# Two attention and two long-convolution layers on one core: all logits summed by heads, the last convolution's tables asked for earlier, and new orders of work

## The chip, the cores and the metric

The kernel runs on one core of a Trainium2 chip. The core has a matrix engine (TensorE, PE; its weight loads are listed apart as PEld), a vector engine (VectorE, DVE), an activation engine (ScalarE, ACT), a general engine (GpSimd, POOL) and a queue engine (SyncE, SP) that issues most transfers. Each works through its own list of instructions in order and waits on semaphores of the others. PE writes to PSUM, from where DVE or ACT copy to SBUF. The metric is the device time of one execution in microseconds.

## The reference

One sequence of 2048 positions and 512 features passes through four layers: attention A, convolution B, A again, B again, each added to its input after a layer norm. Both A layers use the same weights, both B layers the same filter.

```python
def _A_ref(x, wqkv, wo):            # 32 heads of 16, window W = 8, dilation 2
    qkv = (x @ wqkv).reshape(B, S, 3, H, Dh)...
    idx = pos[:, None] - off[None, :]           # s, s-2, ..., s-14
    logits = einsum("bhsd,bhswd->bhsw", q, kg) * scale    # masked where idx < 0
    o = einsum("bhsw,bhswd->bhsd", softmax(logits), vg)
    return o.reshape(B, S, D) @ wo
def _B_ref(u, ...):                 # K[d, l] = Re sum_n C B dt exp(dt A l)
    y = irfft(rfft(u, 2L) * rfft(K, 2L))[:L]    # causal convolution over L = 2048
    return y + u * Dskip
x = x + A(layernorm(x)); x = x + B(layernorm(x)); x = x + A(layernorm(x)); x = x + B(layernorm(x))
```

## The kernel before

**Stages.** `k_gen` builds the filter K on DVE (tables of powers, L1119) and PE (products, L1277), and beside it runs the first attention's front: layer norm of the input (`apply`, L195 and L197), transposes (L1205), projections of q and k (L1215). `LayerA.core` is an attention; it runs twice. `FftB` is a convolution by a two-stage transform with matmuls; it runs twice, the first time also with the transform of the filter itself. Between the first convolution and the second attention lies a second front (layer norm, transposes L271, projections L282 and L223).

**Order.** Every stage takes its order from a string of letters or tokens written out by hand: `ORDERK` for `k_gen`, `CORE0` and `CORE1` for the two attentions, `ORDER0` and `ORDER1` for the two convolutions, `ORDERF` for the end of the first convolution mixed with the second front. One letter issues one operation with all its instructions, on whichever engines it has; since the engines have lists of their own, a string is the interleaving of four lists. Under `tc.manual_schedule(engines=...)` the listed engines keep the written order. Before the change there were several such stretches, one for a stage, with a few calls between them (`open_mid`, `front_w`).

**An attention.** Rows lie in 16 row blocks `a` of 128; four of them make a block `q`. Letters of the core: `v` values of one row block (four matmuls of 512 columns, L398, ACT copy L400), `q` a projection of q (L223, copy L225), `m` a product q times eight shifted k's on DVE (`mult`, L342, 128 x 4096), `l` its sum over the 16 features of a head on PE (`lsum`), `x` the maximum (L414, DVE), `e`, `r`, `n` exponent, logarithm of the sum and normalised exponent (L430, L443, L453, ACT), `T` a turn (L459 to L461), `P` the weights times eight shifted v's on DVE (L472, 128 x 4096), `S` or `V` the sum of these over the taps on PE (L497 in 64-row halves, L487 whole), `O` the output projection with the residual (L506, L508), `b`, `d`, `a`, `f`, `t` the next layer norm (`a` applies it to a row block on DVE, `f` on ACT).

**Two ways to sum logits.** `NCOL` says how many of the four blocks `q` are summed by heads: the 32 columns of `ind` are the weights, the product is the moving operand, and four such matmuls fill the 32-partition quarters of the PSUM tile `L` (L350, 8 matmuls of 512 columns for one `l`). The result has heads on partitions, so after the normalised exponent the weights must be turned with 8 transposes into the upper half of the same PSUM tile and copied by ACT. The other blocks take the product as weights, 32 of them for one `l`, each with `ind8` of 8 columns as the moving operand (L354); the result has rows on partitions and needs no turn. `NCOL = (2, 2)`: blocks 0 and 1 by heads, 2 and 3 the other way. There are two `L` tiles and two tiles of products (`prod`), so the third product waits until the first has been summed; `ex`, which holds the exponents and is the turn's input, has one tile.

**The end of the filter table.** `ORDERK` ends with the first three logit products of the first attention (`X`, into the freed table tiles) and their sums (`Z`); the fourth product is `m` in `CORE0`, and its tile lies where the tables were. The letters `z` and `y` of `ORDERK` apply the layer norm, on engines named in `ENGK`. `KROWS` names the engines of the eight copies that bring the filter into the layout of the convolution (L1459, letters A to H of `CORE0`).

**The second front.** In `ORDERF`, `v` and `z` are the last pieces of the first convolution's inverse transform into `x_sb` (matmuls with the twiddles `g2`, then an evacuation, L911 to L937), `h`, `H`, `a`, `p`, `n` the statistics and layer norm of a block (`h` half of the columns, `H` all, `a` aggregates, `p` the power on ACT, `n` applies), `T` its transposes, `E` an evacuation of half of them, `P` and `Q` projections, `x` the shifted copy of k. Letter A or D behind it is ACT or DVE. The rest of the front (four P, three Q, the last shifted copies) is issued by four events 0 to 3 in `CORE1`.

**The convolutions.** `K` and `U` are the first transform stage of filter and input (L811, evacuation L800), `k` and `u` the second (L818, L800 and L869), `m` the product of spectra on DVE (L857), `y` or `Y` the first inverse stage (L883 or L887), `w` and `v` the last. The filter's spectra go to `kf_dram` during the first convolution and are read back in the second into a ring of tiles: seven of its own (`kf_ring`) and three more in tiles that the attention frees (`kx`, the rest of `w2_sb`). `w2_sb` holds the second stage's weights, 32 transfers of 128 KB for each convolution, in the place of `kT_ext` and the weights (letter `w`).

## Time and profile before

| | before |
|---|---|
| time, median of 3 runs | 395.1 us (394.6 to 396.57) |
| span of the profiled execution | 393.9 us, first to last instruction |
| DVE busy | 372.8 us in 449 instructions |
| ACT busy | 331.1 us in 568 |
| PE busy | 324.1 us in 6451 matmuls |
| granted PE clock | 0.999 over the span |
| moved by DMA | 54.18 MB, mean 138 GB/s |

The profile is of one execution; its span is 1.2 us shorter than the runs' median, which also holds what lies before the first and behind the last instruction. Times in a view by stage are from the span's start. In a view of groups, a row reads: line, engine, operation, output from input, shapes and count, then busy time and mean ns of one, then the engine's idle time ahead of them and what ended it. In a view in order of time a row reads: start, length, engine, line, operation, count, and in brackets the idle time before it with its releaser; "issue" means that the profile shows nothing that it waited for. Neighbouring instructions of one engine overlap by some tens of ns, and PE's matmuls by more, so the start of the next instruction tells better what one costs than its length.

### The profile page before, as it was taken

The page shows a single profiled execution, that of the slowest core. Times are in us where ns is not written, and L with a number is a line of the kernel's source. Part 1 is how long each engine was busy: PE and PEld are TensorE (multiplying, and loading weights), DVE is VectorE, ACT ScalarE, POOL GpSimd, SP SyncE. Part 2 cuts the span into 40 slices and gives each one's busy share as a digit, 9 for nine tenths or more (in the row PEclk, how much of TensorE's full clock was granted, in tenths as well). Part 3 has the DMA queues.
Part 4 walks back from the last instruction along what each step waited for, and adds up shares of the span by engine and source line. Part 5 has one row for each costly group of instructions (what it writes and reads, how often), then busy time and mean ns, then how long its engine had stood idle before and what let it go on. Part 6 is the DMA issues. An engine that isn't in the chain of part 4 may idle for free.

```text
span 393.9 us, 14769 instructions
## 1 busy us (share of the span) xinstructions
PE 324.1 (82%) x6451; PEld 231.5 (59%) x6499; DVE 372.8 (95%) x449; ACT 331.1 (84%) x568; POOL 65.5 (17%) x97
## 2 busy tenths in 40 slices
PE   3000258999999999999998899999999999998894
PEld 2000116756734676766887888543456676677894
DVE  6999999999989999999999989979999999989984
ACT  7999999997558799899999998574666779889992
POOL 9402960000280000010731201100000020000000
PEclk9999999999999999999999999999999999999999
DMA  7953810414027556277678634820253057604525
GB/s 209 396 155 50 83 53 3 106 28 108 9 66 198 128 168 176 61 228 235 215 265 300 216 110 110 300 62 2 73 141 96 3 170 222 195 13 155 171 68 152
DMA packets 68303, 54.18 MB, mean 138 GB/s; under 512 B 33545, under 2 KB 58670, under 8 KB 67982
## 3 DMA queue, kind: packets, MB, share of 16 engines
q1 hardware_dynamic: 66566, 48.70, 42.7%
q0 software_dynamic: 1664, 4.52, 3.1%
q8 instruction: 51, 0.84, 0.9%
q14 instruction: 14, 0.11, 0.1%
q10 hardware_dynamic: 8, 0.00, 0.0%
HBM read 30.15 MB, written 13.24 MB: 110 GB/s over the span
## 4 chain that ended last, share of the span: by engine, by line
PE 49%; DVE 21%; ACT 19%; issue 5%; DMA 2%; SPq 2%; POOL 1%; DVEq 0%; ACTq 0%; POOLq 0%
PE pq L398 7%; PE po L497 5%; PE pq L508 4%; PE pq L223 4%; PE pk L1277 3%; DVE A_t L1119 3%; ACT ub L869 3%; DVE B_t L1119 3%; PE L L354 3%; PE pp L282 3%; ACT a1s L800 3%; PE pp L1215 2%; DVE t L857 2%; SPq L596 2%; PE L L350 2%
## 5 line engine op out<-in xcount | busy, mean ns | idle before, releaser
L472 DVE TENSOR_TENSOR pav<-attn,v_ext 128x4096 bf16<-128x4096 bf16 (+1 forms) x34 | 72.3, 2160 | 0.3 <-DMA v_ext<-v_ext 0.3
L342 DVE TENSOR_TENSOR prod<-qT,kT_ext 128x4096 bf16<-128x4096 bf16 x29 | 65.6, 2288 | 3.0 <-PE L L350 2.1
L1119 DVE TENSOR_TENSOR A_t<-A_t,pow_t 128x1024 bf16<-128x1024 bf16 (+4 forms) x46 | 38.2, 873 | 0.2
L1205 PE MATMUL pt<-ident,x_blk 128*128 128x128 bf16 x64 | 6.0, 241 | 39.4 <-ACT x_blk L195 39.4
L508 PE MATMUL pq<-wop,oT 128*128 128x512 bf16 x121 | 31.5, 379 | 2.4 <-issue 1.9
L497 PEld LDWEIGHTS <-pav 64*128 64x128 bf16 x1728 | 26.9, 95 | 9.9 <-DVE pav L472 3.3
L869 ACT CAST ub<-pb 128x1024 bf16<-128x1024 f32 x32 | 32.6, 1110 | 0.0
L1215 PE MATMUL pp<-xnT,kT_ext 128*128 128x512 bf16 x88 | 25.5, 413 | 7.3 <-ACT xnT L1208 4.3
L818 PE MATMUL pb<-a1s,w_sb 128*128 128x64 bf16 x768 | 27.4, 193 | 3.8 <-ACT ub L869 1.4
L398 PE MATMUL pq<-wv,xnT 128*128 128x512 bf16 x123 | 30.0, 379 | 0.5 <-ACT kgs L1285 0.3
L497 PE MATMUL po<-ident,pav 64*128 64x64 bf16 x1728 | 29.9, 190 | 0.6 <-ACT oT L499 0.2
L400 ACT CAST v_ext<-pq 128x512 bf16<-128x512 f32 x32 | 18.7, 586 | 13.5 <-PE pq L398 11.1
L800 ACT CAST a1s<-pb 128x1024 bf16<-128x1024 f32 x29 | 28.5, 1063 | 1.2 <-PE pb L811 1.2
L1205 PEld LDWEIGHTS <-x_blk 128*128 128x128 bf16 x64 | 4.6, 107 | 41.3 <-ACT x_blk L195 40.2
L818 PEld LDWEIGHTS <-w_sb 128*128 128x128 bf16 x768 | 25.1, 98 | 6.0 <-issue 4.0
L178 POOL TENSOR_TENSOR ln_rstd<-ln_rstd,ln_mh 128x4 f32<-128x4 f32 x2 | 4.0, 1995 | 120.1 <-DVE ln_rstd L177 66.9
L1277 PEld LDWEIGHTS <-A_t 128*64 128x64 bf16 (+1 forms) x512 | 21.7, 103 | 3.8 <-DVE A_t L1119 0.2
L800 DVE CAST a1s<-pb 128x1024 bf16<-128x1024 f32 x19 | 22.5, 1220 | 1.4 <-PE pb L811 1.0
L1277 PE MATMUL pk<-B_t,A_t 128*64 128x84 bf16 (+1 forms) x512 | 23.5, 201 | 0.2
L223 PE MATMUL pq<-xnT,kT_ext 128*128 128x512 bf16 x85 | 22.6, 379 | 0.9 <-issue 0.5
L225 ACT CAST qT<-pq 128x512 bf16<-128x512 f32 x24 | 14.0, 585 | 9.8 <-PE pq L223 9.5
L398 PEld LDWEIGHTS <-xnT 128*128 128x128 bf16 x128 | 11.9, 97 | 15.3 <-issue 2.4
(264 smaller groups left out, 919.9 us busy)
## 6 DMA issues: line engine op xcount, KB each, us to landing
w_sb<-w_dram SPq DMA_DIRECT2D x64, 128.0 KB, 3.0
w_dram<-xnT SPq DMA_DIRECT2D x1, 4096.0 KB
kf_ring<-kf_dram SPq DMA_DIRECT2D x13, 256.0 KB, 3.8
kf_ring<-kf_dram SPq DMA_DIRECT2D x26, 128.0 KB, 3.6
v_ext<-v_ext SPq DMA_DIRECT2D x4, 784.0 KB, 6.1
x_blk<-in_A_x_dram SPq DMA_DIRECT2D x4, 512.0 KB, 4.7
kT_ext<-in_A_wqkv_dram SPq DMA_DIRECT2D x4, 512.0 KB, 9.2
x_sb<-in_A_x_dram SPq DMA_DIRECT2D x4, 512.0 KB, 6.3
```

What stands on the lines that cost most here:

```text
L223: nc.tensor.matmul(pq[:], lhsT=self.wqk[:, dt, ft * P:(ft + 1) * P], rhs=self.xnT[:, dt, q * 512:(q + 1) * 512], start=(dt == 0), stop=(dt ...
L342: nc.vector.tensor_tensor(pr, self.qT[q][:, ft].unsqueeze(1).to_broadcast([P, W, 4, P]), kap, ALU.mult)
L398: nc.tensor.matmul(pp[:], lhsT=xnT[:, dt, a * P:(a + 1) * P], rhs=wv[:, dt, :], start=(dt == 0), stop=(dt == NDT - 1))
L472: nc.vector.tensor_tensor(pv[:, i], attn[:, n % 4].unsqueeze(2).to_broadcast([P, W, DH // parts, H]), vap, ALU.mult)
L497: nc.tensor.matmul(po[:, h, 0, i * nt + ft, :], lhsT=pvf[rows, i, w, ft * P:(ft + 1) * P], rhs=ident[rows, rows], start=(w == 0 and ft + i ...
L508: nc.tensor.matmul(pw[:], lhsT=oT[:, ftp, :], rhs=self.wo[:, ftp, :], start=False, stop=(ftp == NDT - 1))
L800: (self.nc.scalar.copy if eng == "act" else self.nc.vector.tensor_copy)(dst, src)
L818: nc.tensor.matmul(p2[:, j, :], lhsT=self.w2[:, ec * EC + j, :], rhs=a1s[:, ec * EC + j, :], start=True, stop=True)
L869: nc.scalar.copy(ub[:], p2)
L1119: return lambda: nc.vector.tensor_tensor(*args)
L1215: nc.tensor.matmul(pps[kind, b, ft][:], lhsT=la.wqk[:, dt, c:c + P], rhs=la.xnT[:, dt, b * 512:(b + 1) * 512], start=(dt == 0), stop=(dt = ...
L1277: nc.tensor.matmul(o, lhsT=lhs, rhs=Bt[:, ri, c * CH + ql].rearrange("p b g -> p (b g)"), start=(not half and j % 4 == 0 and ri == 0), sto ...
```

## The change

1. `NCOL` becomes (4, 4): all blocks of both attentions are summed by heads, so `CORE0` and `CORE1` have four `T` instead of two.
2. The last convolution's `g2` and its seven own spectrum tiles are allocated before the second attention on the other side of SBUF, and four events of `CORE1` (0 to 3, behind its second product) issue their 22 transfers. The convolution starts with these seven as loaded.
3. `load_w2` is cut into four parts of eight transfers (letter `W`); in both cores the four stand together.
4. The rest of the second front, four events before, becomes 13 single letters with an engine each (`RKEYS`, `RROWS`); `qproj1`, `front_k` and `front_ext` take the engine.
5. All six order strings are new. Counted by letter: `ENGK` has no application on DVE (two before), `KROWS` has one copy on ACT (three before), `ORDERF` evacuates four transposed halves on ACT (two before), `CORE0` has 5 `a` and 3 `f` (6 and 2), 15 `S` and 1 `V` (13 and 3), `CORE1` 4 `a` and 8 `f` (7 and 5), 16 `S` and no `V` (14 and 2). The evacuations of `ORDER0` and `ORDER1` keep their totals for each engine.
6. One `manual_schedule` for DVE, ACT, PE and SP covers the whole program; POOL is added for `k_gen` as before.

```diff
 ORDERK = """
-sbiCCiCisCGiCbiMsaibsCbMiibMcMsTibMGicGMMbasMGiGibTMTMbsGGTabbiTTiaTsicGTbbacTiTibcGsTMTGiaGaMlM
...
-kUTzkzUkTxkTKttkKkUkUkpKekekxKUUpkkKqxpKUqUUxUkUoEUUkpQkUKkpxUUoxpUXpxXKopxxZXZZ
...
+UqKzkQkqTzKzkUzUkqpxQtUUtpUexkKpUUxUkUeUkKkUxkKpkxEppKoUxoUkkUKoEkUpxkKpXZxXXxZZ
...
 ORDERF = """
-yD h00 h01 yA YA v101A v100A v110A v111A h10 z12A a0 p0 v113A h11 a1 p1 z02A S z03A n0D T0 n1G E00D
-v103D E01A P03 H2 a2 T1 P01 E10D p2 E11D Q00 n2G H3 P00 a3 P02 P11 P12 p3 T2 E21D E20D P10 P13
-P22 P20 n3D T3 E31A P23 P21 E30D x1
+yD yA h00 YA v100A v101A v110A v111A v113A h01 h10 a0 v103D p0 z12A n0D S h11 z02A T0 E01A a1 p1
+z03A E00D n1G P03 P01 H2 P02 T1 E10A a2 p2 E11D P00 P11 P10 Q00 n2G H3 a3 T2 E21D E20A p3 n3D P13
+P22 P12 P21 T3 E30A x1D E31D P23 P20
...
 CORE0 = """
-vmvvvvqlvmxvlmemvvrclvnlmqTlqmxmvvelvvvvcmlqcPlSPrqOmncml1VTxPPqeSmr2lqP4OlSOSm5PqOP3S7lmOSnlPOx
-VPeOPSPrOSnPO6SObbP9SwOP8SPdBHOVaOPfSEdObatSaCaAfataGDFO
+vvmvcmvlcxqmlvevlvmmvrclnqvcmlmTvqlvvvvxvevqlmP1rqlnPq4mmlVxm2TqOPlSm5lS3l7PqOPSPeOSrOmPnSlOTxSP
+eOSbPrOSnO8PSP6TO9SdbOPSOPSPPOWWWWSffdOSbPtaaEODGSAaBCfOtaFHa
 CORE1 = """
-0m1l2ml3mqvvmvllqvmqvxqelmlvmmvvqrlnqlmTvmxPPvlvvqvvqvmlmvqlqelmSrqnxmPSPqTOSOSlePOlPmrSOSnmOOPl
-bSlPSPwOxdfPVaePOSraPOnVabPOSPdOSOPSbPOSfaOftSdafaaftO
+CDABFGJKImmN0123EqHllvLmmvvlmqvlvvqmxqlmlvvemqlrvnlmqxTqmvlvvvmPvvPvqllqemqlmqrSmnOSTxPeOPlSlrSO
+qPSnOPmmbTSPOllWWWWOSxdeOPrSfnPSfPOSPTOSbPOPSdfOPSOSfPbaOSPftOfSdtffaaaO
...
-NCOL = (2, 2)
-ENGK = dict(..., y="AAAAAAAAAADA", z="DAAA", ...)
+NCOL = (4, 4)
+ENGK = dict(..., y="AAAAAAAAAAAA", z="AAAA", ...)
 STATD = (3,)
-KROWS = "DADAADDD"
+RKEYS = "ABCDEFGHIJKLN"
+RROWS = "AADDAADAAADDD"
+KROWS = "DDDDADDD"
...
+def kf_read(nc, kc, kf_dram, n):
+    g, ec = divmod(n, NEC)
+    nc.sync.dma_start(kc[0::2], kf_dram[g, ec])
+    for r in range(2):
+        nc.sync.dma_start(kc[1::2, r], kf_dram[g, ec, :, 1 - r])
...
     def open_mid(self):
-        nc.sync.dma_start(self.g2[:], self.g2_dram[:])
         if t:
-            for n in (4, 3):
-                kr = self.c_mid.enter_context(tc.tile_pool(name=f"b{t}_kf{n}", bufs=1, reuse_waits="tile"))
...
+            self.nkf = len(self.ring)
+            self.kf = dict(enumerate(self.ring))
             self.ring += self.extra
...
+    ctx.enter_context(tc.manual_schedule(engines=MAN))
...
-    with tc.manual_schedule(engines=MAN_ALL):
+    with tc.manual_schedule(engines={ET.Pool}):
         C = k_gen(...)
...
+    ring_ctx = ExitStack()
+    g2p = ring_ctx.enter_context(tc.tile_pool(name="b1_g2", bufs=1, side="right", reuse_waits="tile"))
+    g2 = g2p.tile([P, 2, 16, P], BF16, name="g2_sb")
+    ring = []
+    for n in (4, 3):
+        kr = ring_ctx.enter_context(tc.tile_pool(name=f"b1_kf{n}", bufs=1, side="right", reuse_waits="tile"))
...
-        ev = {"w": lambda: la.load_w2(w2_dram),
-              "0": last(("P", 3, 0), ("P", 3, 1), ("x", 0), ("x", 2), ("P", 3, 2), ("Q", 0, 1), ("e", 0), ("Q", 0, 2)),
-              "1": last(("P", 3, 3), ("Q", 0, 3)), "2": last(("e", 1), ("e", 2)), "3": last(("e", 3))}
+    ev = la.w2_loads(w2_dram)
+    ev |= {"0": lambda: nc.sync.dma_start(g2[:], g2_dram[:]), "1": lambda: ring_loads(0, 1), "2": lambda: ring_loads(2, 3),
+           "3": lambda: ring_loads(4, 5, 6)}
+    rest = (("P", 3, 0), ("P", 3, 1), ("x", 0), ("x", 2), ("P", 3, 2), ("Q", 0, 1), ("e", 0), ("Q", 0, 2),
+            ("P", 3, 3), ("Q", 0, 3), ("e", 1), ("e", 2), ("e", 3))
+    for c, e, (op, *ix) in zip(RKEYS, RROWS, rest):
+        ev[c] = lambda e=e, op=op, ix=ix: front[op](*ix, dict(A="act", D="dve")[e])
+    la.core(x_sb, u, lnp, CORE1, ev)
```

More of the change, by code (lines that the diff above doesn't have):

```diff
@@ L217, in __init__, with qproj1 @@
         self.st = [dict() for _ in range(4)]
-    def qproj1(self, q, ft, qT, ps, tag):
+    def qproj1(self, q, ft, qT, ps, tag, eng="act"):
         nc = self.nc
@@ L846, in kf_load @@
         kc = self.ring[n % len(self.ring)]
-        sync.dma_start(kc[0::2], self.kf_dram[g, ec])
-        for r in range(2):
-            sync.dma_start(kc[1::2, r], self.kf_dram[g, ec, :, 1 - r])
+        kf_read(self.nc, kc, self.kf_dram, n)
         self.kf[n] = kc
@@ L1487 @@
     fb.open_mid()
-    with tc.manual_schedule(engines=MAN):
-        late["."] = lambda: None
-        fb.run(ORDER0, u, k=kp, late=[late[c] for c in LATE0.split()])
+    late["."] = lambda: None
+    fb.run(ORDER0, u, k=kp, late=[late[c] for c in LATE0.split()], more={"g": lambda: nc.sync.dma_start(fb.g2[:], g2_dram[:])})
     fb.c_mid.close()
@@ new lines @@
+    fb.run(ORDERF, None, more=front)
+    la.front_close()
+    fb.c_ps.close()
+    fb.c_grp.close()
+    krctx.close()
+    ring_ctx = ExitStack()
[4 more added lines that the diff above has]
+        kr = ring_ctx.enter_context(tc.tile_pool(name=f"b1_kf{n}", bufs=1, side="right", reuse_waits="tile"))
+        kr = kr.tile([P, n, 2, DQG, EC], BF16, name=f"kf_ring{n}")
+        ring += [kr[:, i] for i in range(n)]
```

128 lines of the change are left out of this document (61 added, 67 removed).

## The prediction

> **What bounds the kernel now.** I read the page first (busy times and the chain of waits), then busy time by stage, then the groups with their shapes kept apart, then the order in time at the places where VectorE (DVE) waits.
>
> ```profile
> PE 324.1 (82%) x6451; PEld 231.5 (59%) x6499; DVE 372.8 (95%) x449; ACT 331.1 (84%) x568; POOL 65.5 (17%) x97
> ...
> PE 49%; DVE 21%; ACT 19%; issue 5%; DMA 2%; SPq 2%; POOL 1%; DVEq 0%; ACTq 0%; POOLq 0%
> ```
>
> DVE is busy for 372.8 of 393.9 us: only 21.1 us of the span are without it. TensorE (PE) carries half of the chain, so the two hand the end to each other. Where the 21.1 us lie is seen by stage (busy columns PE, PEld, DVE, ACT, POOL):
>
> ```profile
> 0.00:10.00 10.00, 3.14 (x25) 2.49 (x25) 6.30 (x20) 7.46 (x15) 9.09 (x35) 1.00 0.77 212
> 10.00:98.00 88.00, 44.26 (x508) 28.71 (x515) 87.44 (x141) 83.08 (x155) 22.80 (x12) 1.00 0.43 109
> 98.00:110.00 12.00, 11.63 (x195) 8.03 (x194) 10.43 (x11) 6.84 (x12) 3.95 (x7) 1.00 0.09 24
> 110.00:185.00 75.00, 72.49 (x1473) 46.17 (x1490) 74.56 (x58) 64.86 (x128) 8.17 (x15) 1.00 0.55 155
> 185.00:240.00 55.00, 50.42 (x1497) 47.08 (x1493) 53.23 (x61) 54.52 (x63) 15.03 (x25) 1.00 0.63 218
> 240.00:262.00 22.00, 21.37 (x175) 13.64 (x176) 19.21 (x59) 15.04 (x30) 3.50 (x4) 1.00 0.59 187
> 262.00:290.00 28.00, 27.58 (x211) 12.38 (x214) 26.83 (x16) 16.72 (x28) 0.00 (x0) 1.00 0.24 62
> 290.00:335.00 45.00, 44.10 (x1056) 30.75 (x1066) 44.43 (x31) 34.09 (x76) 2.94 (x1) 1.00 0.40 118
> 335.00:349.00 14.00, 12.75 (x328) 7.99 (x331) 12.97 (x27) 11.56 (x28) 0.00 (x0) 1.00 0.44 140
> 349.00:390.00 41.00, 36.34 (x1011) 34.23 (x1005) 37.44 (x35) 36.95 (x41) 0.00 (x0) 1.00 0.41 125
> 390.00:393.90 3.90, 0.00 (x0) 0.00 (x0) 0.00 (x0) 0.00 (x0) 0.00 (x0) 0.93 0.26 77
> ```
>
> DVE idle, length less busy: start 3.70, filter table 0.56, its end 1.57, first attention 0.44, first convolution 1.77, second front 2.79, second attention 1.17 + 0.57 + 1.03, last convolution 3.56, last store 3.90. In the table, both attentions and the first convolution DVE is the bound; in the second front and the first 28 us behind it PE is (21.37 of 22, 27.58 of 28). An order can win back only the middle, 1.57 to 1.03 in this list: 9.3 us.
>
> **Work moved between engines.** Counting letters in the old and new orders gives these moves, priced by groups of the same shape:
>
> ```profile
> L197 DVE TENSOR_SCALAR xnT<-x_sb,ln_rstd,ln_nb 128x512 bf16<-128x512 bf16 x16 | 6.3, 415 | 0.1
> ...
> L273 DVE COPY xnT<-pt 128x1024 bf16<-128x1024 bf16 x6 | 3.9, 678 | 1.2 <-PE pt L271 1.2
> ...
> L1459 DVE COPY k_perm<-k_rl 128x1024 bf16<-128x1024 bf16 x5 | 2.0, 421 | 0.0
> ...
> L195 ACT ACTIVATE xnT<-x_sb,ln_nb,ln_rstd 128x512 bf16<-128x512 bf16 x8 | 6.4, 814 | 0.0
> ...
> L1459 ACT COPY k_perm<-k_rl 128x1024 bf16<-128x1024 bf16 x3 | 3.1, 1044 | 0.2 <-DMA w_sb<-w_dram 0.2
> ...
> L273 ACT COPY xnT<-pt 128x1024 bf16<-128x1024 bf16 x2 | 2.0, 1014 | 0.5 <-PE pt L271 0.5
> ```
>
> Two normalisations of the first front go from DVE to ACT (-2 x 0.415 on DVE, +2 x 0.814 on ACT), two filter copies the other way (+2 x 0.421, -2 x 1.044), two transposed-block copies of the second front to ACT (-2 x 0.678, +2 x 1.014), one normalisation at the end of the first attention and three at the end of the second to ACT (-4 x 0.415, +4 x 0.814). Summing all blocks by heads adds two turns per attention, four ACT copies (+4 x 1.01, the L461 row below). Convolution evacuations only change places: each order keeps its total for DVE and ACT. DVE: -0.83 + 0.84 - 1.36 - 1.66 = -3.0 us. ACT: +1.63 - 2.09 + 2.03 + 3.26 + 4.04 = +8.9 us.
>
> **The logits on PE.** Starts of the weight loads show what a group costs: one (block, ft) by heads is 8 matmuls of L350, one in the old form of blocks 2 and 3 is 32 of L354; L459 is a turn; L497 and L487 are the two forms of the sum over taps.
>
> ```profile
> 282.05 0.12 PEld L350 LDWEIGHTS <-ind 128*32 128x32 bf16 x8
> ...
> 282.60 0.11 PEld L424 LDWEIGHTS <-nident 128*128 128x128 bf16 x2 [0.42 <-issue]
> ...
> 284.00 0.12 PEld L350 LDWEIGHTS <-ind 128*32 128x32 bf16 x8 [0.42 <-issue]
> ...
> 284.68 0.45 PEld L459 LDWEIGHTS <-ex 128*128 128x128 bf16 x8
> ...
> 285.34 1.01 ACT L461 COPY attn<-L 128x1024 bf16<-128x1024 bf16 x1 [0.53 <-PE L L459]
> ...
> 293.50 1.07 PEld L354 LDWEIGHTS <-prod 128*128 128x128 bf16 x32
> ...
> 294.49 0.55 PEld L398 LDWEIGHTS <-xnT 128*128 128x128 bf16 x4
> ```
> ```profile
> 319.61 1.04 PE po L497 x64
> ...
> 323.89 1.80 PE po L487 x32
> ```
>
> By heads: 282.05 to 282.60, 0.55 us. Old form: 293.50 to 294.49, 0.99. The next user of the array waits 0.42 with its load after each L350 (in the 0.55), and 284.00 shows 0.42 ahead of it too. If all of that leading wait were lost, a group would cost 0.97 and the exchange give 0.02; if none, 0.44. I take 0.37, since most of the leading 0.42 passes while earlier matmuls still stream. 16 groups: -5.9 us (bounds -0.3 and -7.0). The new core orders make 4 of the 5 whole-block sums into halves: 4 x (1.04 - 1.80) = -3.0. Turns: +4 x 0.45 = 1.8. PE: -7.1 us, half in each attention.
>
> [...]
>
> What PE's 7.1 us bring is another matter: blocks 2 and 3 are summed from 293 us on in the second attention, and from there to 335 us DVE idles 0.57. PE's shortage, 240 to 290 us, keeps its matmuls.
>
> **The places where DVE waits.** The end of the filter table:
>
> ```profile
> 106.64 1.67 PE L398 MATMUL pq<-wv,xnT 128*128 128x512 bf16 x6 [0.26 <-ACT kgs L1285]
> ...
> 108.25 0.61 PE L350 MATMUL L<-A_pr,ind 128*32 128x512 bf16 x8
> ...
> 109.78 2.29 DVE L342 TENSOR_TENSOR prod<-qT,kT_ext 128x4096 bf16<-128x4096 bf16 x1 [1.57 <-PE L L350]
> ```
>
> The fourth product cannot start before the third logit sum has been read, and that sum stands behind values of V (L398) that the code writes after all three sums: order was not kept across the two separately scheduled stretches. With one schedule over all, sums 2 and 3 come first, and DVE waits for one group (0.55) instead of 1.57. Gain 1.1, bounds 0 and 1.57 (the V products behind then come 1.7 us later on a PE that is full, which can give it all back).
>
> The second front, where PE sets the pace until the first product at 262 us:
>
> ```profile
> 244.18 0.88 PEld L271 LDWEIGHTS <-xn 128*128 128x128 bf16 x15 [0.31 <-DVE xn L197]
> ...
> 246.07 0.53 PEld L282 LDWEIGHTS <-kT_ext 128*128 128x128 bf16 x3 [0.51 <-issue]
> ```
>
> Now T0 follows all inverse-transform pieces and then PE runs dry, 0.31 + 0.51. The new order puts n0 ahead of the second block's statistics and T0 ahead of z03, which fills the hole. Gain 0.8; bounds -1.0 (E01, E10, E20 and E30 on ACT take 1.014 instead of 0.678, 0.34 x 4 = 1.3 later if nothing covers it) and 2.8 (all of DVE's idle). DVE's 1.36 saved here I count at nothing, because it waits here anyway.
>
> **Loads asked for earlier.** The transfer queue of SP, and what uses the spectra:
>
> ```profile
> 245.75 0.34 SPq L770 DMA_DIRECT2D g_sb<-g_dram  x1
> ...
> 255.75 0.59 SPq L849 DMA_DIRECT2D kf_ring<-kf_dram  x1
> ...
> 281.46 0.67 SPq L403 DMA_DIRECT2D v_ext<-v_ext  x1
> ```
> ```profile
> 257.35 1.06 PE L271 MATMUL pt<-ident,xn 128*128 128x128 bf16 x16
> ```
> ```profile
> L857 DVE TENSOR_TENSOR t<-ub,kf_ring 128x2048 bf16<-128x2048 bf16 x13 | 15.1, 1221 | 0.0
> ```
>
> The twiddles and most of the first seven spectrum tiles are already asked for at 245.75 to 256 us, and the products that use them never wait (0.0). Price 0. Behind these 22 issues in SP's queue stands the shift of v_ext for the first tap products; at 0.59 each they last 13 us, and held back until the last transposes of the front (257.35 to 258.41, whose input lies where g2 now goes) they end by 272, nine before 281.46. w_sb in four parts costs the same 32 issues, called together.
>
> **The sum**, against this execution's 393.9 us: table -0.8 (two normalisations; bounds -0.8 and +0.8, as ACT is busy 83.08 of 88 there and gets 1.6 more); its end -1.1; first attention +0.4 (two filter copies in, one normalisation out; bounds -0.4 and +1); first convolution 0 (idle 1.77, chain unchanged; bounds -1 and +1); second front -0.8; second attention -1.25 for three normalisations and -0.7 of its 1.74 idle before 335 (bounds -3.0 and +1.5); last convolution 0 (bounds -1 and +1). Total -4.25: 389.6 us of span. The runs' median is 395.1, 1.2 above this span, so **390.8 us**.
>
> **Rivals.** *More is won:* PE's relief lets the order close all middle idle outside the convolution, 9.3 - 1.8 = 7.5, plus 1.6 of DVE work (0.8 + 0.8): 395.1 - 9.1 = 386.0. For it: most of these waits are for PE. Against: 4 us of it lie before 290, where PE gets nothing off. *Nothing is won:* the front and the table's end stay as they are and the ACT work added lies before rows that DVE needs; 394.5. For it: ACT gains 8.9 us and stands at 84%. *Slower:* the turn of blocks 2 and 3. Their weights went straight from the exponent to the products; now 8 transposes and a copy come between, from 284.68 to 286.35 in the rows above, 1.67 us. The new order leaves one or two tap products between turn and use. It decides when PE or ACT reaches the turn more than one product late; then all four lie open, 4 x 1.67 = 6.7 on top of the forecast: 397.5. Against it: two logit tiles and the order give T2 one or two products' lead, T3 one.
>
> **Chances.** Forecast (388.5 to 393) 0.48, more 0.16, nothing 0.17, turn exposed 0.15, other losses of the new order 0.04. A measurement here tells a change from none at about 0.5%, 393.1 to 397.1. Faster 0.64, same 0.17, slower 0.19. The range 385 to 398.5 takes in the bounds of the terms on the likely side and the turn; the forecast's own is 388.5 to 393.
>
> **What would show it.** L354 gone, 256 matmuls of L350, DVE busy near 369.8 and ACT near 340; the product after the third sum waiting about 0.6; PE without a hole after T0; kf_ring products still at 0.0. Wrong: DVE idle above 2 us ahead of the tap products of rows 8 and 12 (turn), ACT as releaser of DVE in the second attention, or DVE's idle total above 21.

## The result and the profile after

The changed kernel takes 393.65 us (median of 10 runs, 392.98 to 394.77) against 395.87 for the kernel before on the same chip (10 runs, 394.6 to 397.29): a ratio of 0.995, 95% interval 0.9932 to 0.9967. It is faster, by 0.5% and not by the 1.1% forecast. The spans of the profiled executions are 392.3 and 393.9 us. The changed kernel's profiled execution took 394.21 us, 0.56 above its median, so the traces, 1.6 us apart, show less of the gain than the medians, 2.2 apart.

The page of the changed kernel, busy times and the chain of waits:

```profile
PE 320.0 (82%) x6224; PEld 217.6 (55%) x6273; DVE 370.5 (94%) x443; ACT 337.4 (86%) x578; POOL 66.5 (17%) x97
...
PE 44%; ACT 27%; DVE 13%; issue 6%; SPq 5%; DMA 2%; POOL 2%; ACTq 0%; DVEq 0%; POOLq 0%
```

DVE's work fell by 2.3 us (3.0 were forecast), ACT's rose by 6.3 (8.9). ACT's part of the chain went from 19% to 27%, DVE's from 21% to 13%. The same stretches as before, by stage (PE, PEld, DVE, ACT, POOL):

```profile
98.00:110.00 12.00, 11.15 (x169) 7.63 (x171) 11.49 (x10) 7.38 (x13) 4.04 (x7) 1.00 0.24 64
110.00:185.00 75.00, 71.03 (x1374) 39.70 (x1391) 73.49 (x61) 65.65 (x130) 10.06 (x15) 1.00 0.54 157
...
240.00:262.00 22.00, 21.84 (x170) 13.65 (x171) 18.28 (x57) 17.18 (x32) 3.50 (x4) 1.00 0.21 68
262.00:290.00 28.00, 27.84 (x190) 11.61 (x192) 27.35 (x17) 16.87 (x28) 0.00 (x0) 1.00 0.50 163
290.00:335.00 45.00, 42.95 (x1030) 25.70 (x1041) 44.76 (x29) 37.45 (x83) 2.94 (x1) 1.00 0.39 117
335.00:349.00 14.00, 12.74 (x317) 8.39 (x319) 12.09 (x26) 12.91 (x28) 0.00 (x0) 1.00 0.36 115
```

At the table's end (98 to 110) DVE's idle fell from 1.57 to 0.51, but in the first attention (110 to 185) it rose from 0.44 to 1.51. From 335 to 349 DVE's work fell by 0.88 and its idle rose from 1.03 to 1.91, while ACT went from 11.56 to 12.91 of 14. The gaps of DVE above 0.12 us, added from 98 us on, are 10.5 us before and 10.6 after: each wait that went came back somewhere else, and what is left as a gain is little more than the work taken off DVE.

Where the time went is seen by following single DVE instructions through both traces (start of each in us; "stage" is the change since the row above):

| DVE instruction | before | after | ahead by | stage | forecast |
|---|---|---|---|---|---|
| first logit product (table done) | 101.31 | 100.59 | 0.72 | -0.72 | -0.8 |
| fourth logit product | 109.78 | 107.99 | 1.79 | -1.07 | -1.1 |
| last tap product of attention 1 ends | 180.63 | 179.76 | 0.87 | +0.92 | +0.4 |
| first normalisation of the second front | 242.81 | 241.66 | 1.15 | -0.28 | 0 |
| ninth logit product of attention 2 | 282.78 | 281.62 | 1.16 | -0.01 | -0.8 |
| last tap product of attention 2 ends | 342.12 | 340.22 | 1.90 | -0.74 | |
| first product of spectra, last convolution | 355.82 | 354.26 | 1.56 | +0.34 | both -1.95 |
| end of the span | 393.89 | 392.34 | 1.55 | +0.01 | 0 |

Rows of the changed kernel in order of time, DVE at the table's end and in the first attention:

```profile
100.59 6.69 DVE L342 TENSOR_TENSOR A_pr<-qT,kT_ext 128x4096 bf16<-128x4096 bf16 x3
...
107.99 4.49 DVE L342 TENSOR_TENSOR prod<-qT,kT_ext 128x4096 bf16<-128x4096 bf16 x2 [0.51 <-PE L L350]
...
120.85 2.29 DVE L342 TENSOR_TENSOR prod<-qT,kT_ext 128x4096 bf16<-128x4096 bf16 x1 [0.59 <-PE L L350]
123.66 2.29 DVE L342 TENSOR_TENSOR prod<-qT,kT_ext 128x4096 bf16<-128x4096 bf16 x1 [0.52 <-ACT v_ext L400]
```

The wait of 1.57 became 0.51, as the order of PE's sums lets one expect; two new waits, 0.59 and 0.52, follow within 16 us, where the kernel before has none. Their cause is behind other engines (POOL, ACT and PE between 107 and 118 us):

```profile
107.00 6.87 POOL L1307 DMA_DIRECT2D kd_dram<-kgs  x12
113.84 1.14 POOL L739 IOTA g_i<- 128x512 int32 x2
...
114.49 1.33 ACT L744 ACTIVATE g_i<-g_i,aux 128x512 int32<-128x512 int32 x2 [1.51 <-POOL g_i L739]
115.73 0.56 ACT L225 CAST qT<-pq 128x512 bf16<-128x512 f32 x1
...
116.35 1.02 PE L398 MATMUL pq<-wv,xnT 128*128 128x512 bf16 x4 [1.23 <-ACT qT L225]
```

POOL writes the filter to DRAM until 113.84 and makes only then the second set of indices; ACT waits 1.51 us for it, the copy of q behind it comes late, and PE stands 1.23 us. The new `CORE0` asks for this angle step (letter `c`) at its ninth place, where the old one had it much later.

At the start and the end of the second attention:

```profile
261.73 0.29 DVE L295 COPY kT_ext<-kT_ext 128x508 bf16<-128x508 bf16 x1 [0.57 <-ACT kT_ext L285]
261.94 2.28 DVE L342 TENSOR_TENSOR prod<-qT,kT_ext 128x4096 bf16<-128x4096 bf16 x1
...
344.68 0.74 DVE L197 TENSOR_SCALAR xnT<-x_sb,ln_rstd,ln_nb 128x512 bf16<-128x512 bf16 x2
...
347.25 2.56 DVE L810 CAST a1s<-pb 128x1024 bf16<-128x1024 f32 x2 [1.27 <-PE pb L821]
```

The first product starts 0.04 us ahead of before (261.98), although the front's last normalisation ended 1.0 ahead: one more shifted copy of k now stands in front of it. And DVE waits 1.27 us ahead of the last convolution (0.82 before; e7 below shows why). Two stretches of 22.9 us up to ACT's last copies, first the kernel before, then the changed one:

```profile
323.40:346.30 22.90, 21.48 (x504) 14.46 (x508) 22.66 (x33) 20.48 (x50) 0.00 (x0) 1.00 0.64 199
```
```profile
321.50:344.40 22.90, 20.96 (x632) 13.99 (x638) 22.36 (x26) 22.43 (x53) 0.00 (x0) 1.00 0.65 200
```

ACT went from 20.48 to 22.43 us of 22.9: it has half a microsecond of slack left. The groups show the two edits with names of their own:

```profile
L865 DVE TENSOR_TENSOR t<-ub,kf_ring 128x2048 bf16<-128x2048 bf16 x13 | 15.2, 1216 | 0.0
...
L461 ACT COPY attn<-L 128x1024 bf16<-128x1024 bf16 x8 | 8.1, 1008 | 0.0
...
L350 PEld LDWEIGHTS <-ind 128*32 128x32 bf16 x256 | 4.7, 94 | 11.5 <-issue 9.5 <-DVE prod L342 0.4
```

256 weight loads for the logits by heads, eight turns whose copies ACT starts without having idled, and products of spectra that never wait for a load. No group of the old form (L354) is left.

### The profile page after: what moved, and what is told of

Same layout as the page of the kernel before. It is cut to its first block, busy times and chain, and to the rows that moved or that the text cites. A ratio compares the mean times of both kernels' runs of the same rounds, so it can differ in the third digit from the quotient of the medians.

```text
span 392.3 us, 14328 instructions
## 1 busy us (share of the span) xinstructions
PE 320.0 (82%) x6224; PEld 217.6 (55%) x6273; DVE 370.5 (94%) x443; ACT 337.4 (86%) x578; POOL 66.5 (17%) x97
## 4 chain that ended last, share of the span: by engine, by line
PE 44%; ACT 27%; DVE 13%; issue 6%; SPq 5%; DMA 2%; POOL 2%; ACTq 0%; DVEq 0%; POOLq 0%
PE pq L398 6%; PE pq L223 4%; ACT a1s L810 4%; PE pp L282 4%; PE pk L1285 3%; PE pp L1223 3%; PE pq L508 3%; PE L L350 3%; PE po L497 3%; ACT ub L877 3%; ACT x_blk L195 2%; SPq L1390 2%; PE pb L891 2%; DVE B_t L1127 2%; ACT ln_junk L145 2%
## 5 line engine op out<-in xcount | busy, mean ns | idle before, releaser
L497 PEld LDWEIGHTS <-pav 64*128 64x128 bf16 x1984 | 31.1, 95 | 12.2 <-issue 5.0
L497 PE MATMUL po<-ident,pav 64*128 64x64 bf16 x1984 | 34.7, 190 | 0.5
L178 POOL TENSOR_TENSOR ln_rstd<-ln_rstd,ln_mh 128x4 f32<-128x4 f32 x2 | 6.0, 2984 | 107.8 <-DVE ln_rstd L177 107.8
L223 PE MATMUL pq<-xnT,kT_ext 128*128 128x512 bf16 x89 | 23.5, 380 | 0.5 <-issue 0.2
L508 PEld LDWEIGHTS <-oT 128*128 128x128 bf16 x128 | 12.3, 98 | 13.8 <-ACT oT L499 2.1
```

The source lines that it names most:

```text
L223: nc.tensor.matmul(pq[:], lhsT=self.wqk[:, dt, ft * P:(ft + 1) * P], rhs=self.xnT[:, dt, q * 512:(q + 1) * 512], start=(dt == 0), stop=(dt ...
L497: nc.tensor.matmul(po[:, h, 0, i * nt + ft, :], lhsT=pvf[rows, i, w, ft * P:(ft + 1) * P], rhs=ident[rows, rows], start=(w == 0 and ft + i ...
L508: nc.tensor.matmul(pw[:], lhsT=oT[:, ftp, :], rhs=self.wo[:, ftp, :], start=False, stop=(ftp == NDT - 1))
```

## Experiments

All runs beside the kernel before on the same chip; ratio of medians with its 95% interval. The changed kernel's is 0.995.

| run | kernel and edit | median us | ratio | span us |
|---|---|---|---|---|
| e1 | changed, index wait later | 393.27 | 0.9936 [0.9915, 0.9957] | 391.6 |
| e2 | changed, two normalisations back on DVE | 394.26 | 0.9963 [0.9943, 0.9983] | 393.0 |
| e3 | before, all blocks by heads | 400.78 | 1.0117 [1.0088, 1.0146] | 398.8 |
| e4 | before, one schedule | 399.04 | 1.008 [1.0049, 1.0112] | 395.8 |
| e5 | changed, four sums whole | 397.55 | 1.004 [1.0016, 1.0064] | 395.2 |
| e6 | changed, loads late | 394.97 | 0.9982 [0.9955, 1.001] | 392.2 |
| e7 | changed, last convolution's old order | 393.62 | 0.9935 [0.9912, 0.9958] | 391.3 |
| e8 | e1 and a shifted copy later | 393.01 | 0.9924 [0.9896, 0.9952] | 391.1 |
| e9 | before, four sums in halves | 395.54 | 1.0009 [0.9988, 1.003] | 395.7 |
| e10 | changed, heads undone | 397.77 | 1.0052 [1.0034, 1.007] | 395.8 |
| e11 | e8, old last order, one more sum in halves | 395.16 | 0.9988 [0.9973, 1.0003] | 395.8 |
| e12 | e11, three loads of x earlier | 394.16 | 0.997 [0.9952, 0.9988] | 392.4 |
| e13 | e8, three loads of x earlier | 392.87 | 0.9925 [0.9897, 0.9953] | 391.1 |
| e14 | e11, that sum whole again | 393.32 | 0.9932 [0.9907, 0.9958] | 391.8 |

Executions of the same code differ: up to the second attention e6 and e7 issue what the changed kernel issues, and their first logit product there comes 0.7 us ahead of its. So medians decide about the whole, and spans of single executions only where a wait can be named.

### Where the order gave time back (e1, e8, e2)

```diff
 CORE0: -vvmvcmvlcxqmlvevlvmmvr...
        +vvmvcmvlxqmlvecvlvmmvr...        (e1, e8)
 CORE1: -CDABFGJKImmN0123...
        +CDABFGJImKmN0123...              (e8 only)
```

> The changed kernel with one letter moved: in the first attention the second angle step (c) stands behind the first block's exponent instead of ahead of the maximum. In the changed kernel's trace ACT waited there 1.51 us for an index table of POOL, PE then 1.23 for a copy of ACT, DVE 0.59 and 0.52. Theory (what the table's end won, 1.06 us, is given back through this wait): ACT's wait for POOL and PE's for ACT vanish, DVE's two waits fall below 0.3 together, the first tap product comes at 128.2 instead of 129.2, the median 0.5 to 1.0 us below the changed kernel's 393.65. Rival (it is given back because 1.7 us of V products now come later on a full PE): DVE still waits about 1.1 us before the first tap product, time unchanged.

DVE in e1, in order of time:

```profile
117.69 4.49 DVE L342 TENSOR_TENSOR prod<-qT,kT_ext 128x4096 bf16<-128x4096 bf16 x2
122.66 2.29 DVE L342 TENSOR_TENSOR prod<-qT,kT_ext 128x4096 bf16<-128x4096 bf16 x1 [0.49 <-ACT v_ext L400]
...
128.20 2.29 DVE L472 TENSOR_TENSOR pav<-attn,v_ext 128x4096 bf16<-128x4096 bf16 x1
```

The wait of 0.59 is gone, the one for v_ext stays; from the fourth logit product to the first tap product e1 takes 20.46 us, the changed kernel 21.21. So the index wait cost 0.75 of the 1.1 us that came back in this stretch; the 0.5 for v_ext has another cause, which was not tried. The median is only 0.38 us below the changed kernel's, where 0.5 to 1.0 were expected: behind this place PE halts for 0.93 us at 145.4 (see the halts below), and attention 1 ends 0.39 sooner.

> A version meant to beat both: the changed kernel with the index wait of the first attention moved later (0.72 us in the experiment on it alone) and, in the second, the shifted copy that needs the front's last inverse piece put behind the first query product and no longer ahead of it. Theory (that copy holds up the first product 0.6 to 0.8 us, and VectorE is the bound for the 28 us behind it): first product of the second attention 0.6 to 0.8 us earlier than in the first of these two, at most half of it left at the end of the second attention, where ScalarE is as late as VectorE; span 390.9 to 391.5. Rival (PE sets those 28 us, so the first product's lead is gone by the next ones): span as with the index wait alone, 391.6 and up.

DVE in e8 at the start of the second attention:

```profile
259.97 0.29 DVE L295 COPY kT_ext<-kT_ext 128x508 bf16<-128x508 bf16 x1 [0.17 <-ACT kT_ext L285]
260.30 2.29 DVE L342 TENSOR_TENSOR prod<-qT,kT_ext 128x4096 bf16<-128x4096 bf16 x1
```

The first product comes at 260.30, 0.87 us ahead of e1's 261.17. At the ninth, 20 us on, 0.13 are left (280.71 and 280.84), which e8 had ahead of the edit already (first normalisation of the front at 240.75 against 240.88). On the mechanism the rival was right: DVE waits there, but PE sets these 28 us, and a DVE instruction that starts earlier only waits later. The span, 391.1, lies in the theory's range by luck: at the end of the second attention e8 leads e1 by 0.14 us, and the rest of its lead of 0.5 arises behind it, where the two have the same code.

```diff
 CORE1: -...SPftOfSdtffaaaO
        +...SPftOaSdtafaaaO
```

> The changed kernel with two normalisations at the end of the second attention (row blocks 6 and 7) back on DVE. Theory as predicted (DVE is the bound, each normalisation counts 0.415 us): last convolution's first product 0.8 us later than the changed kernel's 354.26. Rival (ACT has no gap from 321 to 344 us in the changed kernel and ends this stage, so the move to ACT won nothing here): that product not later, up to 0.8 earlier, ACT's busy time 1.6 us less between 335 and 349 us.

e2 puts 0.83 us of work (2 x 0.415) back on DVE and takes 1.6 off ACT, whose busy time from 335 to 349 us is this (the changed kernel has 12.91):

```profile
335.00:349.00 14.00, 12.38 (x301) 7.98 (x304) 12.52 (x27) 11.34 (x26) 0.00 (x0) 1.00 0.42 133
```

From the first logit product of attention 2 to the first product of spectra e2 takes 92.50 us, the changed kernel 92.32. In these two executions the edit costs 0.18 and not 0.83: at this end ACT is nearly as late as DVE, and a normalisation moved there wins almost nothing. (From the last tap product to the first product of spectra alone e2 takes 14.22 us; five runs with the changed code there and no halt take 13.87 to 14.04.) The first product of spectra comes 0.66 later than the changed kernel's, near the 0.8 of the theory, but 0.48 of that arose before the edit, in the first attention, where PE halts for 1.29 us at 146.3 (see the halts below). The medians lie 0.6 us apart, and the intervals of the two ratios overlap: they do not decide between 0.18 and 0.83.

### Single parts in the old order (e3, e4, e9)

```diff
-NCOL = (2, 2)
+NCOL = (4, 4)                    (e3; a T behind the third and fourth n of both cores)
```

> The kernel before with all four blocks summed by heads and two more turns in each attention, nothing else. Theory (PE's relief lies where DVE is the bound): PE busy with L354 gone, ACT 4.1 us busier, DVE's busy time as before, time within 0.8 us of before. Rival (the turns of blocks 2 and 3 lie open): DVE idle ahead of the tap products of row blocks 8 and 12, 1.67 us each, 3 to 7 us slower. Second rival (PE's relief is on the path): 2 to 4 us faster.

DVE in e3, in both attentions:

```profile
161.62 2.29 DVE L472 TENSOR_TENSOR pav<-attn,v_ext 128x4096 bf16<-128x4096 bf16 x1 [0.90 <-ACT attn L461]
...
174.38 2.29 DVE L472 TENSOR_TENSOR pav<-attn,v_ext 128x4096 bf16<-128x4096 bf16 x1 [0.96 <-ACT attn L461]
...
337.60 2.29 DVE L472 TENSOR_TENSOR pav<-attn,v_ext 128x4096 bf16<-128x4096 bf16 x1 [1.23 <-ACT attn L461]
```

Here the turns lie open: 0.90, 0.96 and 1.23 us of wait for the turn's copy, with more behind them; attention 1 ends 3.84 us later than before, the span grows by 4.9. The forecast's rival, the exposed turn, is a real mechanism of the old order. In the new one no tap product waits for L461.

```diff
+    ctx.enter_context(tc.manual_schedule(engines=MAN))     (e4; the later stretches fall away)
```

> The kernel before with one schedule over the whole program, nothing else; the last convolution's twiddles and spectrum tiles then stand in SP's list behind the second attention, as they are written. Theory: DVE's wait at the table's end falls from 1.57 to about 0.5 us, and the last convolution's first products wait for the spectra (13 us of issues and 4.5 MB from about 345 us), 2 to 10 us slower than before. Rival (the convolution's first stage, some 7 us of evacuations, hides the transfers): at least 0.8 us faster than before.

DVE in e4:

```profile
108.68 4.49 DVE L342 TENSOR_TENSOR prod<-qT,kT_ext 128x4096 bf16<-128x4096 bf16 x2 [0.51 <-PE L L350]
114.65 1.23 DVE L414 TENSOR_REDUCE mx<-L 128x128 bf16<-128x1024 f32 x1 [1.48 <-PE L L325]
```

One schedule alone makes the wait at the table's end 0.51, as in the changed kernel: the explanation of that wait holds. But DVE now waits 1.48 for the logits ahead of its first maximum, and the first tap product comes 0.65 later than before. The slower time, 3.3 us by the medians, was expected for another reason, products waiting for late spectra; no DVE instruction of e4 waits for a load, so that the expected range was met by luck. Of the further losses, the 0.8 in the first convolution has a halt of PE in it (0.71 us, until 193.13), for which DVE waits 0.61; the 0.9 between the second attention and the first product of spectra has no cause that these runs show.

```diff
 CORE0: -VPeOPSPrOSnPO6SObbP9SwOP8SPdBHOVaOPf...
        +SPeOPSPrOSnPO6SObbP9SwOP8SPdBHOSaOPf...   (e9; in CORE1 blocks 8 and 10)
```

> The kernel before with only one part of the change: four of its five sums over taps taken in halves (blocks 7 and 13 of the first attention, 8 and 10 of the second), PE -3.0 us. In the changed kernel, whole sums put back cost 2.9 us of span. Theory (PE's time counts in full in the attentions, before as after, and the rest of the change together gives nothing): span 391.0 to 392.4. Rival (only the new order is so tight on PE; in the old one VectorE is the bound): span within 0.5 us of 393.9, each attention's end within 0.3.

The median is that of the kernel before, 395.54 to 395.56. The first attention ends as early as before (180.51, with its table 0.12 ahead), the second wins 0.36 between ninth logit product and last tap product. The profiled execution, 1.9 us above the runs' median, shows PE halting twice in the first convolution (0.95 and 0.76 us), where the edit has nothing. So in the old order PE's relief alone, 3.0 us of its work, is worth 0 and 0.36 us in the two attentions and nothing in the median. The edit changes the number of PE instructions, but whether the other executions hold such halts, and how far halts took back the 0.36, was not shown.

### Single parts taken out of the new order (e5, e10, e6, e7)

```diff
 CORE0 blocks 7, 13; CORE1 blocks 9, 10: -S +V       (e5)
-NCOL = (4, 4), four T                               (e10)
+NCOL = (2, 2), two T
```

> The changed kernel with four sums over taps again as whole blocks (blocks 7 and 13 of the first attention, 9 and 10 of the second), as the kernel before had them: PE's time goes up by 4 x 0.76 = 3.0 us and nothing else changes. PE had been relieved by this part and by the sums by heads. Theory (VectorE and ScalarE set the end of both attentions, PE's relief there is worth nothing): within 0.3 us of the changed kernel's span of 392.3, at most 0.4 later at the end of either attention. Rival (PE is a bound in the attentions, so its relief paid for part of the gain): each attention ends 0.8 to 1.5 us later, span 394 to 395.

(The kernel before has its whole sums of attention 2 at blocks 8 and 10.) PE and DVE of e5 in attention 2:

```profile
330.68 1.95 PE L487 MATMUL po<-ident,pav 128*128 128x128 bf16 x32
```
```profile
332.74 2.29 DVE L472 TENSOR_TENSOR pav<-attn,v_ext 128x4096 bf16<-128x4096 bf16 x1 [0.70 <-PE po L487]
```

The theory falls. 3.0 us of PE work cost 2.9 us of span, and by the ratios 0.9% (3.6 us). Attention 1 ends 0.68 later, and the first convolution starts 1.0 later; attention 2 takes 0.78 longer to its last tap product, 1.38 to the first product of spectra. A halt of PE in the first convolution (0.54 us, at 235.6) is in the span as well. In the new order PE is as much the bound of the attentions as DVE.

> The changed kernel with blocks 2 and 3 of both attentions summed again by positions (L354) and without their two turns; all else, the order too, as in the changed kernel. PE +5.9 for the logits, -1.8 for the turns; ScalarE -4.0 for the copies. Theory (PE's time counts in full, as the whole sums showed): each attention ends 1 to 2 us later, span 394.5 to 396.5. Rival A (the turn in the path eats what PE is spared): span 392.0 to 393.0. Rival B (ScalarE is the bound at the second attention's end, and four copies fewer help it): the second attention ends earlier and the span falls under 391.8.

The same answer: 3.5 us of span, attention 1 ends 1.36 later and attention 2 takes 1.41 longer to its last tap product for some 2.05 us of PE work in each; 0.36 come back at the end, perhaps because ACT has fewer copies (a little of rival B); runs of the same code differ there by 0.17. Two halts in the first convolution (0.51 and 0.81 us) are in this span too. e9 and these two together: the relief brings next to nothing in the old order, and the new order cannot do without it. It has spent the slack. What it bought with it, piece by piece, these runs do not show.

```diff
 CORE1: -CDABFGJKImmN0123EqH...PvvPvqllqem...
        +CDABFGJKImmNEqH...PvvPv0123qllqem...        (e6)
 ORDER1: the old one                                 (e7)
```

> The changed kernel with the four groups of loads (g2 and the seven spectrum tiles) asked for behind the last value projection of the second attention, near 290 us, and not as it begins. Theory (those loads are hidden anyway; where they are asked for was worth nothing): all milestones of VectorE within 0.3 us of the changed kernel's, no VectorE wait on a spectrum tile, span 392.0 to 392.8. Rival (asking early pays): the last convolution's first products wait, its middle starts 1 us or more later, span above 393.3. Second rival (asking early costs, since 22 issues stand ahead of the shift of v_ext in SP's queue): the first tap products of the second attention come 0.3 us or more earlier and the span falls under 391.9.

No product of spectra waits, and the first tap product of attention 2 keeps its distance to the stages before it; in that the theory holds, and the span, 392.2, is what it named. But between 296 and 308 us, with the loads in flight, PE stops in the middle of a sum and DVE waits 0.61 for it; stage and PE rows of e6:

```profile
296.00:308.00 12.00, 11.21 (x300) 6.96 (x302) 11.99 (x6) 8.95 (x19) 0.00 (x0) 1.00 0.95 323
...
306.62 0.79 PE L497 MATMUL po<-ident,pav 64*128 64x64 bf16 x42
308.06 0.50 PE L497 MATMUL po<-ident,pav 64*128 64x64 bf16 x22 [0.65 <-issue]
```

The DMA share is 0.95 there. The median is above e7's, whose code is the same up to this place, by 1.35 us. Asked for later than before the change, the loads cost something, though not by making their users wait.

> The changed kernel with the last convolution's order of the kernel before; nothing else differs. In the changed kernel VectorE waits 1.71 us once near 379 and its last work comes 1.75 us earlier than before, while the end of the second attention comes 1.90 earlier. Theory (the new last order gives nothing): last work and span within 0.4 us of the changed kernel's 392.3. Rival A (the new order costs, its one long wait stands for five short ones): span 391.3 to 391.9. Rival B (the old order was laid out for a later ScalarE and costs here): span 392.8 to 394.

DVE in e7 ahead of the last convolution:

```profile
345.88 4.83 DVE L810 CAST a1s<-pb 128x1024 bf16<-128x1024 f32 x4 [0.82 <-PE pb L821]
```

The old last order begins with an evacuation by DVE (`UD`), the new one with one by ACT (`UA`), the late engine there. With the old one DVE waits 0.82 us (also before the change and in e11 and e12), with the new one 1.27 (also in e1, e2, e5, e6 and e8). From the last tap product to the first product of spectra e7 takes 13.63 us, e11 and e12 13.63 and 13.64, against 14.04 in the changed kernel and 13.70 before. By the end little of that is left: 0.7 of e7's lead of 1.0 us over the changed kernel's execution was there before the last convolution, and from the last tap product to the end of the span it takes 51.81 us, while e1 and e8, both with the new order, take 52.16 and 51.79. The medians, 393.62 and 393.65, decide: on the whole the new last order gives nothing and costs nothing that can be measured.

### The halts of PE (e11, e12, e13, e14)

> A version meant to beat both: the changed kernel with the index wait later, the last shifted copy behind the first query product, the one sum over taps left whole (block 0 of the first attention) in halves, and the last convolution's order of the kernel before. Expected from the single runs: -0.7 to -0.9 for the first two, -0.4 for the last, and for the halves -0.76 if PE's time counts there, 0 if VectorE is the bound in the first blocks: span 389.8 to 391.0.

The joined version lost what it should have won: 395.16, 2.15 us above e8. Its trace has DVE waiting 0.96, 0.88 and 1.04 us for PE in attention 1, and PE standing still for 1.56 us in the middle of 64 equal matmuls with nothing that the profile shows to wait for:

```profile
143.05 0.61 PE L350 MATMUL L<-prod,ind 128*32 128x512 bf16 x8
143.80 0.70 PE L497 MATMUL po<-ident,pav 64*128 64x64 bf16 x36
146.06 0.58 PE L497 MATMUL po<-ident,pav 64*128 64x64 bf16 x28 [1.56 <-issue]
...
150.32 2.29 DVE L472 TENSOR_TENSOR pav<-attn,v_ext 128x4096 bf16<-128x4096 bf16 x1 [0.96 <-PE po L497]
```

Such halts are in most of the runs. The changed kernel's page has a DMA queue named "instruction" with 49 packets, 0.80 MB together; in its trace 146 to 328 PE and PEld instructions start between the starts of two neighbouring packets (165 to 357 before), those on semaphores counted too. By the packets' records there are, from 98 us on, 27 halts of PE above 0.28 us with releaser "issue" in the runs e1 to e14, and every one ends 1.2 to 1.95 us after a packet of that queue has landed. In the changed kernel's attentions the packets start 3.65 us or more apart, so that a halt's end would fall into that stretch of 0.75 us by chance about once in five times, or less often. The kernels before and after the change have no such halt in their profiled executions: the longest idle of PE with releaser "issue" from 98 us on is 0.16 us in both. In e11 the queue brings none from 130 to 143.4 us; its two views of the DMA queues, 131 to 143 and 143 to 145 us:

```profile
DMA packets 1852, 2.69 MB, mean 224 GB/s; under 512 B 177, under 2 KB 1468, under 8 KB 1852
...
q1 hardware_dynamic: 1852, 2.69, 78.1%
...
q1 hardware_dynamic: 80, 0.03, 9.1%
q8 instruction: 1, 0.02, 3.7%
```

The packet comes when the data have passed. Two runs test, without touching a single PE instruction, whether its lateness stops PE:

```diff
-ev = {("v", 0): lambda: x_load((0,)), ("v", 1): lambda: x_load((1, 2, 3)), ...
+ev = {("v", 0): lambda: x_load((0, 1, 2, 3)), ...            (e12 on e11, e13 on e8)
```

> The joined version with three of the four loads of x (0.5 MB each) asked for behind the first shift of v_ext, near 125 us, where the transfer queues are nearly empty, and no longer near 134, where they are full until 142. No TensorE instruction changes. Theory (TensorE's halt of 1.56 us at 144.5 to 146.06 is a late packet of its own instructions, which stood behind those loads): the packet that landed at 144.5 lands before 142, the halt falls under 0.4 us, VectorE's wait of 0.96 at 150.3 goes, and the median falls by 0.7 us or more from 395.2. Rival (the halt comes from the matmuls' own inputs or from the order): the halt stays within 0.3 us of 1.56 at the same instruction.

The same stretch of 8 us in e11 and e12 (last columns: clock, DMA share, GB/s), and PE in e12:

```profile
134.00:142.00 8.00, 6.88 (x113) 3.15 (x112) 8.00 (x5) 7.35 (x10) 0.00 (x0) 1.00 1.01 305
```
```profile
134.00:142.00 8.00, 6.88 (x113) 3.15 (x112) 8.00 (x5) 7.35 (x10) 0.00 (x0) 1.00 0.51 129
...
143.04 0.61 PE L350 MATMUL L<-prod,ind 128*32 128x512 bf16 x8
143.79 1.11 PE L497 MATMUL po<-ident,pav 64*128 64x64 bf16 x64
145.00 0.61 PE L350 MATMUL L<-prod,ind 128*32 128x512 bf16 x8
```

Identical work on all engines, DMA share 1.01 against 0.51, and the halt is gone. The packets around it, from the queue's records (start, landing, PE and PEld instructions from the start of the one before, those on semaphores counted too):

```text
e11   129.09  130.02         e12   131.66  132.68
      143.36  144.54  +437         138.83  139.78  +244
      147.16  148.63  +147         144.86  146.22  +298
```

DVE's wait of 0.96 is gone too. Attention 1 ends 2.8 us earlier, the span falls by 3.4, the median by 1.0 (the profiled execution of e11, 397.55 us, was the slowest of its 12). The theory's forecasts hold: the packet lands at 139.78, before 142, and halt and wait are gone. That the packet holds PE's instructions is the author's reading of the queue's name and of these times; no view shows what is in it. e12 still halts near 169, 235 and 383 us.

> The same move of the three loads in the version with the index wait and the shifted copy later (e8), whose TensorE halts 0.53 us at 145.9 without costing VectorE a wait. Theory (late instructions): the halt goes, the span stays within 0.3 us of 391.1, because VectorE had no wait there. Rival: the halt stays.

In e13 no halt is left, and as expected nothing is won, since DVE did not wait for that one: span 391.1, median 392.87, ratio 0.9925. It is the fastest version of the study, with e8 at its side.

> The joined version with the sum over taps of block 0 whole again: 64 TensorE instructions fewer, 0.76 us more of TensorE time; it differs from e8 only in the last convolution's order. Theory (that sum in halves brought the late instructions): median 392.4 to 393.4, span 390.5 to 391.4, the halt at 146 back to some 0.5 us. Rival (the old last order costs the 2 us here): median above 394.5.

393.32 and 391.8, the halt at 146 back to 0.51: the one more sum in halves had brought the loss of e11, not the old last order. The span is 0.4 above the expected range and 0.7 above e8's; another halt of PE, 0.85 us at 340.1, lies there.

## Why the prediction was right or wrong

**Right:** the table (-0.8; measured -0.72); its end (-1.1; -1.07, with the wait at 0.51 where 0.6 was named, and e4 shows it to be the schedule); the loads at price 0, which the 0.0 of their products shows; the turn hidden by the new order and exposed without it (e3); the exchange on PE, where a group by heads again takes 0.55 between weight loads.

**Where it failed: the size of the second attention's term**, -1.25 for three normalisations and -0.7 of idle; measured -0.74 to the last tap product and +0.34 behind it, 1.55 of the 2.7 us by which the span missed its forecast. Of the three normalisations two lie ahead of the last tap product, and they were won: from the ninth logit product on DVE's work falls from 58.67 to 57.94 us. The idle was not: it is 0.67 us there before and after, and the rest of the 1.74 lay ahead of the ninth product, where PE sets the pace (e8: a lead of 0.87 us shrinks to 0.13). The third normalisation lies behind the last tap product, where ACT is nearly full (22.43 of 22.9 us) and e2 shows 0.18 us for two in its trace. The row "335.00:349.00", with ACT busy 11.56 of 14, stood in the prediction and was not used. The +0.34 itself comes from the new order of the last convolution, which was put at 0: with the old order the stage takes 13.63 us (e7), 0.07 less than before. By the end of the span the two orders cannot be told apart.

**The second front's -0.8.** The table's -0.28 and -0.01 have to be read together, because the mark between them moved: the new `ORDERF` puts the first normalisation ahead of matmuls of the inverse transform that stood in front of it before (from there to the ninth product PE has 22 of them, 2.6 us, and had 17, 1.8 us). These fill the hole behind T0 (PE's idle from 240 to 262 fell from 0.63 to 0.16), and the time from the mark to the ninth product stays what it was. From the end of attention 1 to the ninth product the kernel before takes 102.15 us and e3, with the same front, 102.46; the changed kernel takes 101.86, and the seven other runs with its front and no halt there (e1, e2, e6, e7, e8, e13, e14) 101.26 to 101.78. So 0.3 to 1.2 us were won, -0.8 lies within, and the profiled execution shows the least of it.

**The first attention's +0.4** became +0.92. Its bound of +1 held, but not its cause: not the filter copies, but an index step moved up to where POOL still writes the filter (e1: 0.75), a wait for which the sum had no term. In e13, without that wait and without a halt, the stretch takes 71.03 us, 0.18 more than before (70.85).

**PE's relief.** "What PE's 7.1 us bring is another matter" was right for the old order (e9) and wrong as a statement about the new one (e5, e10): the sum had no term for PE in the attentions. With four whole sums back (e5), DVE idles 1.36 us and not 0.67 between the ninth logit product and the last tap product of attention 2, and the stretch takes 59.39 us, no less than before (59.34): without that relief the gain of DVE's work there is lost. The rival "nothing is won" had part of the mechanism, ACT work ahead of rows that DVE needs, and the measured time lies between it and the forecast. Two of the signs of being wrong came: DVE's idle is 21.8 us, above 21, and ACT releases DVE in the second attention (0.57 us ahead of its first product's shifted copy of k, 0.32 ahead of the tenth product), though it did so before the change too.

**The base.** The forecast started from 395.1 us, a median of 3 runs; 10 runs beside the changed kernel gave 395.87. So 0.8 of the 2.85 us between 390.8 and 393.65 is the base and not the change.

## What to carry to other kernels

Where three engines are each busy above 80% and share the chain, price a move of work with the receiver's idle time in that very stretch, not with the giver's saving: in the traces, a normalisation was worth 0.4 us in one place and 0.1 in another. When an operation is moved up in a hand-written order, look at what its producer on another engine is doing at that time. And before believing that an edit costs or wins a microsecond on PE, look for halts with releaser "issue" and at the DMA share before them: the form of one sum, 64 PE and PEld instructions more or fewer, made a halt 1.56 or 0.51 us (e11, e14), the time of three loads removed it (e12), and e9, which has its edit in the attentions, halts for 0.95 and 0.76 us in the first convolution.

## What the runs showed of the hardware that was not expected

The DMA queue named "instruction" moved 49 packets, 0.80 MB, while the changed kernel ran, on the same 16 engines as the data. In e11, where 437 PE and PEld instructions started between two of its packets that stood 14.3 us apart, behind 2.69 MB of data, PE stopped for 1.56 us, and moving 1.5 MB of loads by some 8 us removed the halt with the same instructions (e12). The form in halves has 128 PE and PEld instructions in 1.04 us, a whole sum 64 in 1.80, so the form that is cheaper by its matmuls goes through its instructions three to four times as fast. And loads that no product waited for were not free: with them in flight, at a DMA share of 0.95 from 296 to 308 us, PE halted for 0.65 us and DVE waited 0.61 for it (e6).
